# One written order of steps replaced by another in a gated recurrence with a feed-forward block

## The chip, the cores and the metric

The kernel runs on one core of a Trainium2 chip. Five engines work side by side, each through its own list of instructions in order: PE (matrix products), DVE and ACT (elementwise work, ACT also functions such as exp and sin), POOL (small elementwise work here) and SP, which issues nearly all DMA transfers. They wait for each other by semaphores. The metric is the time of one execution in microseconds (us); seven runs of the kernel before have a median of 464.03 us (462.85 to 464.76).

## The reference

Inputs are q, k, v and a complex gate (a_re, a_im) for 4 batches, 8 heads, 768 positions of 48 numbers. For each head a state of 48 x 48 complex numbers is carried over the positions; its output goes through a feed-forward block that closes with a layer norm and a second product.

```python
mag = np.sqrt(a_re * a_re + a_im * a_im)
scale = np.minimum(mag, 0.999) / (mag + 1e-06)
a_re_n, a_im_n = (a_re * scale, a_im * scale)
for t in range(S):
    new_re = ar * S_re - ai * S_im
    new_im = ar * S_im + ai * S_re
    S_re, S_im = (new_re + kv, new_im)        # kv: outer product of k[t] and v[t]
    y[:, :, t] = einsum('bhd,bhde->bhe', q[:, :, t], S_re)
# x: y as (3072, 384)
h = x @ w_in                                  # 3072 x 1024
sm = softmax(h); solu = h * sm
ln = (solu - mean) / sqrt(var + 1e-06) * g_ln
out = ln @ w_out                              # 3072 x 384
```

The weights w_in, w_out and the gain g_ln come as 64-bit floats and are converted on the core.

## The kernel before

The 768 positions are cut in six blocks of 128, and a block of one batch is a *chunk*: 24 chunks, numbered block by block. Two chunks that follow each other form a *group* (12 groups), which shares the preparation of the gates. Nothing in the kernel is a plain loop over engines' work: each piece of work is a named step (a small function that issues one to some hundred instructions), all steps are put in a dictionary `steps` under their name and number, and four written lists say in which order they are issued: `START`, then `EVEN` and `ODD` in turn for the chunks 2 to 19, then `END`. As each engine works through its instructions in the order of issue, the lists set the order on every engine, SP's queue of DMAs included. In the lists `up0:-1` is the step `up0` of the chunk before the current one, and `clamp:g2` that of the group two after the current chunk's. A step is taken out of the dictionary when it is issued; one that is already gone, or isn't there for this number, is passed over.

```python
for n in range(2, NC * B - 4):
    for s in (ODD if n % 2 else EVEN).split():
        nm, i = s.split(":")
        go(nm, n // GB + int(i[1:]) if i[0] == "g" else n + int(i))
```

The steps, by engine and with the line of their main instruction:

- Of a group, the size of the gate: `load_ar`, `load_ai` (SP, L649); `clamp` (DVE, L735); `inverse` (ACT, L740); `ratio`, `tangent` (DVE, L746 to L752); `square`, `secant`, `fourth` (ACT); `size` (DVE, L765); `eps` (ACT); `lnm` (DVE, L772) writes the logarithm `f_lr`; `total0/1` (PE, L777) sums it over the positions; `grow0/1`, `decay0/1` (ACT, L781, L784); `last` (SP, L788) takes the last row of the decays away as `f_ends`; `ends` (DVE and POOL), `turn_ends` (PE), `tot` (DVE). `ks0/1`, `qs0/1` (DVE) scale k and q.
- Of a group, the angle: `trig` (ACT loads tables), `angle` (ACT, L817), `on` (DVE, L822), `phase0/1` (PE, L831), `nearest0/1` (ACT), `part0/1` (DVE, L838, then ACT), `cos`, `sin` (ACT; `sin` also sends one row on by a DMA of SP), `exp` (ACT loads tables).
- Of a chunk: `k2`, `q2` (DVE, L881) double k and q with cos and sin; `kqb` (DVE, L890) and `kqt0` (SP, four DMAs, L895) turn them; chunks 0 and 1 are turned by PE and ACT instead (`kt`, `kT`, `qt`, `qT`). `score0/1` (PE, L937), `mask0` (DVE, L941), `values` (PE, L969), `carry` (PE, L977) and `add` (DVE, L986) give the output `f_y` and the next state.
- Of a chunk, feed-forward: `turned_x` (ACT), `up0/1` (PE, L1009), `exp0` (ACT, L1014), `solu0` (DVE, L1018), `blocks` (DVE, L1037) and `away` (SP, four DMAs, L1043) turn the result; chunks 0, 1, 2 and 23 are turned by PE and ACT (`zt`, `zT`). `centred`, `norm` (POOL), `spread` (ACT, L1054), `down0/1` (PE, L1068), `scale` (ACT, L1073), `store` (SP, L1078).
- Of the weights: `fetch` (SP, L680) brings one of 14 pieces (0 to 5 of w_in, 512 wide; 6 to 13 of w_out, 384 wide), `raised` (ACT) and `convert` (DVE) make 32-bit floats of it; `gain`, `mean` (PE) and `centre` (DVE) fold g_ln and the mean into w_out. `again` (SP) reads a piece once more and `inspect` (DVE) looks at it, for a check on the inputs' range. After `END` comes `verdict`, which gathers these checks in one flag.

Buffers bind the order too. Two PSUM banks in turn serve `total`, `phase`, `turn_ends` and the turns by PE; `values` and `carry` share one bank, which `turned_x` or `add` frees; `up` has one pair of banks, freed by `exp0` and `solu0`; `down` has one, freed by `scale`. The pieces of the weights share six buffers; the results of `kqb` and of `blocks` have one buffer each.

Of the kernel before, what the change touches and what calls it, by code (L numbers as in the profile page):

```python
# [512 lines left out]


START = """
load_ar:0 load_ai:0 clamp:0 fetch:8 fetch:2 fetch:0 fetch:1 inverse:0 ratio:0 raised:8 raised:2 tangent:0
square:0 secant:0 convert:2 size:0 fourth:0 eps:0 fetch:5 convert:8 raised:0 load_k:0 raised:1 lnm:0 total0:0
load_q:0 load_ai:1 convert:1 grow0:0 decay0:0 total1:0 ks0:0 decay1:0 grow1:0 convert:0 trig:0 angle:0 qs0:0
load_ar:1 last:0 fetch:13 raised:5 fetch:3 phase0:0 ks1:0 nearest0:0 convert:5 phase1:0 nearest1:0 part0:0
part1:0 ends:0 load_q:1 cos:0 sin:0 turn_ends:0 exp:0 fetch:4 clamp:1 k2:0 load_v:0 qs1:0 tot:0 kt0:0 q2:0  # L520
inverse:1 kT0:0 qt0:0 kt1:0 qT0:0 k2:1 raised:3 qt1:0 ratio:1 kT1:0 load_vr:0 qT1:0 raised:13 kt0:1 fetch:10
tangent:1 square:1 q2:1 score0:0 kT0:1 score1:0 qt0:1 secant:1 raised:4 convert:3 mask0:0 values:0 size:1
convert:13 qT0:1 turned_x:0 fetch:6 fetch:7 fourth:1 kt1:1 fetch:9 raised:6 convert:4 kT1:1 raised:9 load_ai:2
eps:1 carry:0 convert:6 fetch:12 raised:10 convert:9 load_vr:1 fetch:11 raised:7 qt1:1 up0:0 add:0 up1:0 lnm:1
qT1:1 convert:10 total0:1 total1:1 carry:1 exp0:0 gain:0 mean:0 decay0:1 score1:1 convert:7 load_k:1 grow0:1
solu0:0 add:1 decay1:1 qs0:1 grow1:1 score0:1 load_ar:2 trig:1 mean:1 angle:1 raised:12 ks0:1 phase0:1 load_k:2
last:1 phase1:1 ks1:1 mean:2 qs1:1 mask0:1 convert:12 nearest0:1 nearest1:1 raised:11 part0:1 part1:1 again:0
values:1 clamp:2 cos:1 mean:3 load_vr:3 ends:1 again:1 sin:1 turned_x:1 exp:1 mean:4 convert:11 again:4
inverse:2 zt0:0 k2:2 mean:5 q2:2 kqb:2 zT0:0 load_ai:3 kqt0:2 k2:3 mean:6 ratio:2 mean:7 tangent:2 q2:3 square:2
secant:2 turn_ends:1 zt1:0 centred:0 spread:0 centre:0 fourth:2 centre:7 load_q:2 up0:1 centre:5 centre:4 up1:1  # L530
zT1:0 score0:2 size:2 eps:2 again:2 kqb:3 exp0:1 load_ar:3 tot:1 kqt0:3 centre:1 score1:2 load_v:1 lnm:2
centre:3 total1:2 centre:6 total0:2 decay1:2 centre:2 norm:0 solu0:1 down0:0 grow0:2 inspect:2 again:6 grow1:2
decay0:2 inspect:0 again:8 zt0:1 trig:2 angle:2 zt1:1 centred:1 spread:1 zT0:1 down1:0 mask0:2 on:2 load_v:2
load_v:3 zT1:1 ks0:2
"""
# [24 lines left out]

# [650 lines left out]
```

## Time and profile before

| what | us |
|---|---|
| median of 7 runs (lowest to highest) | 464.03 (462.85 to 464.76) |
| the profiled execution | 462.84 |
| its span, first to last instruction | 461.0 |
| PE busy, share of the span | 408.0, 88% |
| DVE busy | 367.3, 80% |
| ACT busy | 283.6, 62% |
| POOL busy | 54.9, 12% |
| mean granted PE clock | 0.983 |
| SP's DMA queue: time of its packets, as a share of 16 engines' span | 67.9% |

The profile is of one execution. An instruction is named by engine, line and the tile that it writes (`f_o` by `down`, `f_h` by `up`, `f_y` by `values`, `f_L` by `total`, `f_d` by `carry`, `f_kb` by `kqb`, `f_zb` by `blocks`). Matrix products overlap, so PE counts as busy nearly always where it has work; the gaps tell more. The chain of work goes back from the last instruction to whatever released each step.

### The profile page before, as it was taken

How to read it: one execution, taken by the hardware profiler on the slowest of the kernel's cores; microseconds unless marked ns; L12 is line 12 of the kernel's file. 1: busy time of each engine (PE TensorE's matmuls, PEld its weight loads, DVE VectorE, ACT ScalarE, POOL GpSimd, SP SyncE). 2: the span in 40 equal slices, each digit the busy share in tenths (PEclk: the TensorE clock that was granted, in tenths of full speed). 3: DMA queues.
4: the chain of work that ended last, by engine and by line, in shares of the span. 5: the costliest groups of instructions: out<-in, count | busy, mean ns of one | idle time of the engine just before them, and what ended most of it. 6: DMA issues, size and time to landing. Idle time of an engine off the chain costs nothing.

```text
span 461.0 us, 11488 instructions
## 1 busy us (share of the span) xinstructions
PE 408.0 (88%) x4764; PEld 275.0 (60%) x4764; DVE 367.3 (80%) x507; ACT 283.6 (62%) x441; POOL 54.9 (12%) x141
## 2 busy tenths in 40 slices
PE   0257985999999999999999999999999999999992
PEld 0125443654566865875775676676676677667771
DVE  5889999595799799799799799799699798753310
ACT  4989966665666656657648648648647746521230
POOL 3000001111111110110111101101102011011110
PEclk9999988899999999999999999999999999999997
DMA  9878959959369858859659669569569566272200
GB/s 253 196 203 224 190 146 216 254 136 205 99 144 192 205 123 175 203 125 207 160 123 228 146 134 204 129 131 225 118 147 211 110 152 147 42 185 75 63 17 26
DMA packets 167709, 72.28 MB, mean 157 GB/s; under 512 B 142176, under 2 KB 155488, under 8 KB 167648
## 3 DMA queue, kind: packets, MB, share of 16 engines
q1 hardware_dynamic: 167504, 71.14, 67.9%
q8 instruction: 39, 0.64, 0.6%
q10 hardware_dynamic: 144, 0.33, 0.2%
q14 instruction: 22, 0.18, 0.1%
HBM read 38.87 MB, written 4.72 MB: 95 GB/s over the span
## 4 chain that ended last, share of the span: by engine, by line
DVE 43%; PE 39%; issue 7%; ACT 4%; DMA 4%; SPq 2%; DVEq 0%; POOL 0%; ACTq 0%
PE f_o L1068 17%; DVE f_kb L890 9%; PE f_y L969 5%; PE f_h L1009 5%; DVE f_kq L881 5%; PE f_L L777 4%; PE f_phase L831 4%; DVE f_zb L1037 4%; DVE f_z L1018 3%; DVE f_att L941 2%; DMA f_q<-in_q_dram 2%; DVE f_lr L772 2%; DVE f_state L987 2%; DVE f_ai L746 2%; PE f_d L977 2%
## 5 line engine op out<-in xcount | busy, mean ns | idle before, releaser
L1068 PE MATMUL f_o<-f_w_out,f_zT 128*128 128x384 f32 x384 | 135.2, 501 | 0.3 <-ACT f_zT L1031 0.3
L1009 PE MATMUL f_h<-f_w_in,f_xT 128*128 128x512 f32 x288 | 131.2, 600 | 0.0
L1068 PEld LDWEIGHTS f_o<-f_w_out,f_zT 128*128 128x128 f32 x384 | 111.2, 295 | 15.9 <-issue 4.3
L1009 PEld LDWEIGHTS f_h<-f_w_in,f_xT 128*128 128x128 f32 x288 | 52.8, 190 | 55.8 <-issue 52.9
L890 DVE STREAM_TRANSPOSE f_kb<-f_kq 128x1536 f32<-128x1536 f32 x22 | 51.6, 2347 | 0.4
L777 PE MATMUL f_L<-f_lr,f_mats 128*128 128x384 f32 x48 | 21.6, 575 | 29.7 <-DMA f_q<-in_q_dram 17.7
L755 ACT ACTIVATE f_ar<-f_x 128x768 f32<-128x768 f32 x12 | 10.1, 842 | 57.2 <-DVE f_x L752 57.1
L1018 DVE SCALAR_TENSOR_TENSOR f_z<-f_h,f_z 128x1024 f32<-128x1024 f32 x24 | 29.2, 1216 | 19.4 <-ACT f_z L1014 19.4
L1037 DVE STREAM_TRANSPOSE f_zb<-f_z 128x1024 f32<-128x1024 f32 x20 | 42.5, 2123 | 0.4
L1014 ACT ACTIVATE f_z<-f_h 128x1024 f32<-128x1024 f32 x24 | 24.4, 1018 | 24.0 <-PE f_h L1009 23.8
L969 PE MATMUL f_y<-f_att,f_v 128*32 128x128 f32 (+1 forms) x384 | 36.7, 275 | 2.1 <-DVE f_att L941 2.1
L838 DVE SCALAR_TENSOR_TENSOR f_f<-f_f,f_phase 128x384 f32<-128x384 f32 x24 | 13.1, 550 | 29.7 <-ACT f_f L834 29.7
L969 PE MATMUL f_y<-f_att,f_vr 128*32 128x128 f32 x384 | 36.5, 275 | 0.0
L937 PEld LDWEIGHTS f_score<-f_kqT 96*32 96x32 f32 x1536 | 28.9, 110 | 10.8 <-issue 10.3
L1054 ACT ACTIVATE f_z<-f_z,f_less 128x1024 f32<-128x1024 f32 x24 | 27.4, 1142 | 13.0 <-DVE f_zb L1037 5.5
L777 PEld LDWEIGHTS f_L<-f_lr,f_mats 128*128 128x128 f32 x48 | 9.0, 211 | 42.3 <-DVE f_lr L772 30.9
L937 PE MATMUL f_score<-f_kqT 96*32 96x64 f32 (+3 forms) x1536 | 31.9, 234 | 1.1 <-DMA f_kqT<-f_kb 1.1
L941 DVE TENSOR_TENSOR f_att<-f_score,f_mats 128x1024 f32<-128x1024 f32 x24 | 29.1, 1211 | 4.3 <-PE f_score L937 4.1
L969 PE MATMUL f_y<-f_kqT,f_state 96*32 96x128 f32 (+1 forms) x640 | 32.3, 272 | 0.0
L969 PEld LDWEIGHTS f_y<-f_att,f_v 128*32 128x32 f32 (+1 forms) x384 | 19.9, 102 | 16.2 <-DVE f_kq L881 6.1
L1003 ACT COPY f_xT<-f_y 128x384 f32<-128x384 f32 x24 | 11.5, 477 | 26.6 <-PE f_y L969 26.6
L1051 POOL TENSOR_SCALAR f_less<-f_sum 128x1 f32<-128x1 f32 x24 | 8.2, 343 | 152.5 <-DVE f_z L1018 152.4
(99 smaller groups left out, 640.4 us busy)
## 6 DMA issues: line engine op xcount, KB each, us to landing
f_kqT<-f_kb SPq DMA_DIRECT2D x88, 192.0 KB, 3.4
f_zT<-f_zb SPq DMA_DIRECT2D x80, 128.0 KB, 2.7
f_raw<-in_moe_w_out_dram SPq DMA_DIRECT2D x16, 384.0 KB, 4.0
f_raw<-in_moe_w_in_dram SPq DMA_DIRECT2D x12, 512.0 KB, 5.3
f_ar<-in_a_re_dram SPq DMA_DIRECT2D x12, 384.0 KB, 6.0
f_ai<-in_a_im_dram SPq DMA_DIRECT2D x12, 384.0 KB, 5.4
f_k<-in_k_dram SPq DMA_DIRECT2D x12, 384.0 KB, 4.2
f_q<-in_q_dram SPq DMA_DIRECT2D x12, 384.0 KB, 4.9
```

Of the source, the lines that this page charges most:

```text
L777: nc.tensor.matmul(out=ps, lhsT=tri, rhs=st["lr"][:, i * DM:(i + 1) * DM], start=True, stop=True)
L881: nc.vector.tensor_tensor(out=t, in0=T["cs", g][:, i * H:(i + 1) * H], in1=heads(T[nm, g][:, i]).unsqueeze(2).to_broadcast([P, H, 2, D]), ...
L890: nc.vector.transpose(out=t, in_=T["kq", c].rearrange("p n h (f j) -> p j (n h) f", j=3))
L937: nc.tensor.matmul(out=scores[r0:r0 + 32, x, r:], lhsT=QK[:, r // 32, x], rhs=QK[:, r // 32:, H + x], start=True, stop=True)
L941: nc.vector.tensor_tensor(out=st["att"].rearrange("p (i u) t -> p i u t", u=2), in0=scores.rearrange("p (i u) t -> p i u t", u=2), in1=mat ...
L969: nc.tensor.matmul(**product)
L1009: nc.tensor.matmul(out=st["h"][:, half * 512:(half + 1) * 512], lhsT=st["xT"][:, c * P:(c + 1) * P], rhs=w_in[:, c, half * 512:(half + 1) ...
L1014: nc.scalar.activation(out=st["z"], in_=st["h"], func=AF.Exp, accum_out=sums[:, n:n + 1])
L1018: nc.vector.scalar_tensor_tensor(out=st["z"], in0=st["h"], scalar=1.0, in1=st["z"], op0=OP.mult, op1=OP.mult, accum_out=st["sum"][:, 0:1])
L1037: nc.vector.transpose(out=st["zb"].rearrange("p s t c -> p s c t"), in_=st["z"].rearrange("p (c f s) -> p s c f", s=4, f=32))
L1054: nc.scalar.activation(out=st["z"], in_=st["z"], func=AF.Square, bias=st["less"], accum_out=st["sum"][:, 1:2])
L1068: nc.tensor.matmul(out=st["o"], lhsT=st["zT"][:, c] if n in SHORT else st["zT"].rearrange("p r t c -> p (r t) c")[:, :, c], rhs=w_out[:, c ...
```

## The change

The four lists are written anew. The functions of the steps, the buffers, the loop and the set of steps stay as they are: both orders issue the same 1173 steps. In the loop, the odd chunk now has the next even chunk's `values` and the next group's `phase` at its end, where these were at the start of the even chunk; `blocks` and `away` of a chunk are followed by its `down` later; `again` and `inspect` of all pieces stand in `ODD`, where they stood partly in `START` and partly in `EVEN`. `START` goes on to `values:2`, `score` of chunk 3 and `phase` of group 2, so that the loop begins and ends that much further on.

```diff
 START = """
-load_ar:0 load_ai:0 clamp:0 fetch:8 fetch:2 fetch:0 fetch:1 inverse:0 ratio:0 raised:8 raised:2 tangent:0
-square:0 secant:0 convert:2 size:0 fourth:0 eps:0 fetch:5 convert:8 raised:0 load_k:0 raised:1 lnm:0 total0:0
-load_q:0 load_ai:1 convert:1 grow0:0 decay0:0 total1:0 ks0:0 decay1:0 grow1:0 convert:0 trig:0 angle:0 qs0:0
-load_ar:1 last:0 fetch:13 raised:5 fetch:3 phase0:0 ks1:0 nearest0:0 convert:5 phase1:0 nearest1:0 part0:0
-part1:0 ends:0 load_q:1 cos:0 sin:0 turn_ends:0 exp:0 fetch:4 clamp:1 k2:0 load_v:0 qs1:0 tot:0 kt0:0 q2:0
-inverse:1 kT0:0 qt0:0 kt1:0 qT0:0 k2:1 raised:3 qt1:0 ratio:1 kT1:0 load_vr:0 qT1:0 raised:13 kt0:1 fetch:10
-tangent:1 square:1 q2:1 score0:0 kT0:1 score1:0 qt0:1 secant:1 raised:4 convert:3 mask0:0 values:0 size:1
-convert:13 qT0:1 turned_x:0 fetch:6 fetch:7 fourth:1 kt1:1 fetch:9 raised:6 convert:4 kT1:1 raised:9 load_ai:2
-eps:1 carry:0 convert:6 fetch:12 raised:10 convert:9 load_vr:1 fetch:11 raised:7 qt1:1 up0:0 add:0 up1:0 lnm:1
-qT1:1 convert:10 total0:1 total1:1 carry:1 exp0:0 gain:0 mean:0 decay0:1 score1:1 convert:7 load_k:1 grow0:1
-solu0:0 add:1 decay1:1 qs0:1 grow1:1 score0:1 load_ar:2 trig:1 mean:1 angle:1 raised:12 ks0:1 phase0:1 load_k:2
-last:1 phase1:1 ks1:1 mean:2 qs1:1 mask0:1 convert:12 nearest0:1 nearest1:1 raised:11 part0:1 part1:1 again:0
-values:1 clamp:2 cos:1 mean:3 load_vr:3 ends:1 again:1 sin:1 turned_x:1 exp:1 mean:4 convert:11 again:4
-inverse:2 zt0:0 k2:2 mean:5 q2:2 kqb:2 zT0:0 load_ai:3 kqt0:2 k2:3 mean:6 ratio:2 mean:7 tangent:2 q2:3 square:2
-secant:2 turn_ends:1 zt1:0 centred:0 spread:0 centre:0 fourth:2 centre:7 load_q:2 up0:1 centre:5 centre:4 up1:1
-zT1:0 score0:2 size:2 eps:2 again:2 kqb:3 exp0:1 load_ar:3 tot:1 kqt0:3 centre:1 score1:2 load_v:1 lnm:2
-centre:3 total1:2 centre:6 total0:2 decay1:2 centre:2 norm:0 solu0:1 down0:0 grow0:2 inspect:2 again:6 grow1:2
-decay0:2 inspect:0 again:8 zt0:1 trig:2 angle:2 zt1:1 centred:1 spread:1 zT0:1 down1:0 mask0:2 on:2 load_v:2
-load_v:3 zT1:1 ks0:2
+load_ar:0 load_ai:0 fetch:9 fetch:13 fetch:5 clamp:0 fetch:11 inverse:0 ratio:0 raised:9 raised:13 tangent:0
+fetch:2 convert:9 square:0 secant:0 size:0 fetch:0 load_k:0 raised:11 eps:0 convert:13 lnm:0 fetch:1 fourth:0
+total0:0 load_ar:1 raised:0 total1:0 raised:5 decay0:0 grow1:0 grow0:0 decay1:0 convert:11 trig:0 angle:0
+convert:5 convert:0 ks1:0 phase0:0 raised:2 phase1:0 last:0 ks0:0 load_q:0 nearest0:0 gain:0 nearest1:0 ends:0
+load_ai:1 load_v:0 convert:2 raised:1 part0:0 part1:0 fetch:7 cos:0 convert:1 qs0:0 turn_ends:0 tot:0 clamp:1
+sin:0 k2:0 exp:0 q2:0 kt0:0 inverse:1 kT0:0 qt0:0 fetch:3 k2:1 fetch:4 qs1:0 ratio:1 kt1:0 load_vr:0 qT0:0
+raised:7 kT1:0 qt1:0 qT1:0 q2:1 carry:1 kt0:1 score1:0 raised:3 fetch:10 convert:7 fetch:6 kT0:1 fetch:12 add:1
+fetch:8 raised:4 score0:0 load_k:1 mask0:0 load_ai:2 kt1:1 tangent:1 load_q:1 qt0:1 values:0 convert:3 qT0:1
+kT1:1 qt1:1 turned_x:0 carry:0 square:1 qT1:1 secant:1 up0:0 raised:6 convert:4 up1:0 raised:8 size:1 load_ar:2
+eps:1 score1:1 load_vr:2 fourth:1 raised:10 score0:1 convert:6 raised:12 convert:8 lnm:1 total0:1 convert:10
+grow0:1 decay0:1 total1:1 load_v:1 grow1:1 mean:0 convert:12 ks0:1 mean:1 mean:2 mean:3 decay1:1 mean:4 exp0:0
+mask0:1 mean:5 trig:1 qs0:1 angle:1 phase0:1 add:0 nearest0:1 phase1:1 solu0:0 nearest1:1 ks1:1 last:1 mean:6
+centred:0 qs1:1 mean:7 values:1 clamp:2 part0:1 part1:1 zt1:0 cos:1 sin:1 centre:0 exp:1 centre:1 load_k:2
+turned_x:1 zt0:0 centre:4 load_vr:1 centre:3 up0:1 inverse:2 up1:1 centre:2 centre:5 centre:7 zT0:0 k2:2
+centre:6 q2:2 ratio:2 spread:0 tangent:2 load_ai:3 zT1:0 kqb:2 square:2 secant:2 kqt0:2 down0:0 size:2 k2:3 q2:3
+down1:0 eps:2 exp0:1 load_q:2 lnm:2 fourth:2 total1:2 total0:2 kqb:3 solu0:1 grow1:2 decay1:2 kqt0:3 ends:1
+score0:2 centred:1 grow0:2 score1:2 decay0:2 turn_ends:1 tot:1 last:2 zt0:1 mask0:2 zt1:1 load_ar:3 values:2
+qs1:2 score0:3 score1:3 trig:2 angle:2 zT0:1 turned_x:2 on:2 ks1:2 zT1:1 mask0:3 phase0:2 norm:0 load_v:2
+spread:1 phase1:2 ks0:2 scale:0 qs0:2 nearest0:2
 """
 EVEN = """
-again:1 values:0 phase0:g1 phase1:g1 qs1:g1 norm:-1 turned_x:0 nearest0:g1 inspect:-1 carry:0 nearest1:g1 qs0:g1
-part0:g1 add:0 load_q:g2 score1:1 last:g1 again:8 scale:-2 part1:g1 score0:1 cos:g1 clamp:g2 sin:g1 exp:g1
-mask0:1 inverse:g2 up0:0 up1:0 load_vr:g1 exp0:0 k2:2 q2:2 kqb:2 load_v:g2 values:1 kqt0:2 ratio:g2 down0:-1
-solu0:0 zt0:0 turned_x:1 blocks:0 carry:1 down1:-1 tangent:g2 away:0
+nearest1:g1 mask0:1 carry:0 part0:g1 ks1:g1 load_q:g2 part1:g1 cos:g1 clamp:g2 up0:0 sin:g1 up1:0 load_k:g2
+add:0 exp:g1 values:1 inverse:g2 k2:2 exp0:0 down0:-1 q2:2 kqb:2 turned_x:1 ratio:g2 solu0:0 tangent:g2
+load_v:g2 square:g2 load_ar:g3 blocks:0 carry:1 secant:g2 size:g2 k2:3
 """
 ODD = """
-square:g2 secant:g2 fourth:g2 ks1:g1 ends:g1 up0:0 load_k:g2 k2:2 q2:2 score0:1 zT0:-1 score1:1 load_ai:g3
-zt1:-1 centred:-1 spread:-1 turn_ends:g1 size:g2 load_ar:g3 scale:-2 eps:g2 kqb:2 add:0 lnm:g2 tot:g1 mask0:1
-zT1:-1 up1:0 kqt0:2 norm:-1 exp0:0 total1:g2 grow1:g2 inspect:1 total0:g2 grow0:g2 store:-2 decay1:g2 solu0:0
-ks0:g2 decay0:g2 store:-3 trig:g2 angle:g2 blocks:0 centred:0 spread:0 on:g2 down0:-1 away:0 down1:-1
+kqt0:1 down1:-2 q2:2 eps:g2 load_ai:g3 up0:0 up1:0 add:0 fourth:g2 centred:-1 zt0:-1 zt1:-1 zT0:-1 away:-1
+norm:-2 scale:-2 again:-4 score0:1 zT1:-1 lnm:g2 store:-3 score1:1 exp0:0 spread:-1 kqb:2 solu0:0 total1:g2
+decay1:g2 total0:g2 decay0:g2 mask0:1 down0:-1 blocks:0 again:-3 ends:g1 grow0:g2 qs0:g2 load_vr:g2 down1:-1
+last:g2 kqt0:2 grow1:g2 centred:0 turn_ends:g1 values:1 trig:g2 inspect:-3 ks0:g2 angle:g2 score0:2 store:-2
+on:g2 spread:0 inspect:-6 tot:g1 score1:2 away:0 norm:-1 phase0:g2 qs1:g2 turned_x:1 scale:-1 phase1:g2
+nearest0:g2
 """
 END = """
-ks1:11 phase0:11 nearest0:11 values:20 norm:19 phase1:11 turned_x:20 part0:11 nearest1:11 score1:21 part1:11
-score0:21 mask0:21 qs0:11 cos:11 load_vr:11 sin:11 up0:20 exp:11 k2:22 scale:18 q2:22 up1:20 down0:19 kqb:22
-exp0:20 kqt0:22 solu0:20 blocks:20 centred:20 spread:20 values:21 turned_x:21 down1:19 norm:20 scale:19 qs1:11
-k2:23 score0:22 score1:22 q2:23 away:20 up0:21 kqb:23 up1:21 mask0:22 values:22 down0:20 kqt0:23 down1:20
-store:19 exp0:21 last:11 turned_x:22 store:18 scale:20 solu0:21 score0:23 score1:23 blocks:21 centred:21
-spread:21 mask0:23 away:21 up0:22 up1:22 values:23 store:20 down0:21 norm:21 exp0:22 solu0:22 turned_x:23
-blocks:22 centred:22 spread:22 down1:21 ends:11 scale:21 away:22 up0:23 up1:23 down0:22 down1:22 exp0:23
-store:21 solu0:23 norm:22 zt0:23 scale:22 zT0:23 zt1:23 centred:23 spread:23 down0:23 norm:23 zT1:23 down1:23
-store:22 scale:23 store:23
+mask0:21 down0:19 nearest1:11 store:18 part0:11 part1:11 cos:11 sin:11 norm:19 k2:22 up0:20 q2:22 up1:20 exp:11
+kqb:22 ks1:11 values:21 exp0:20 down1:19 solu0:20 turned_x:21 kqt0:22 score0:22 k2:23 q2:23 kqb:23 up0:21
+scale:19 blocks:20 kqt0:23 score1:22 up1:21 mask0:22 exp0:21 score0:23 centred:20 away:20 solu0:21 score1:23
+values:22 mask0:23 blocks:21 centred:21 spread:20 down0:20 turned_x:22 norm:20 up0:22 store:19 down1:20
+spread:21 scale:20 up1:22 exp0:22 values:23 away:21 down0:21 solu0:22 turned_x:23 ends:11 blocks:22 down1:21
+up0:23 norm:21 up1:23 away:22 scale:21 store:20 down0:22 centred:22 exp0:23 solu0:23 zt0:23 spread:22 centred:23
+zT0:23 store:21 down1:22 zt1:23 norm:22 scale:22 down0:23 zT1:23 spread:23 down1:23 norm:23 store:22 scale:23
+store:23
 """
```

## The prediction

> **What bounds the kernel now.** I read the page's busy table first, then the busy times of stretches cut at every fourth `f_L` matmul (step `total`), then the chain of work, then the SP queue in order of time. Busy shares alone do not settle it:
>
> ```profile
> PE 408.0 (88%) x4764; PEld 275.0 (60%) x4764; DVE 367.3 (80%) x507; ACT 283.6 (62%) x441; POOL 54.9 (12%) x141
> ```
>
> The stretches (columns: stretch, length, busy of PE, PEld, DVE, ACT, POOL, granted clock, DMA share, GB/s) split the run into a start, nine pairs of chunks, an end and a tail:
>
> ```profile
> 0.00:78.93 78.93, 42.93 (x451) 23.83 (x451) 67.52 (x119) 63.42 (x97) 6.19 (x18) 0.96 0.83 204
> 78.93:116.19 37.26, 34.96 (x369) 19.98 (x370) 27.42 (x40) 23.05 (x36) 5.46 (x11) 0.94 0.85 199
> 216.19:249.54 33.35, 32.67 (x417) 22.97 (x417) 30.17 (x41) 21.45 (x34) 5.11 (x11) 1.00 0.76 169
> 249.54:282.95 33.41, 32.67 (x417) 22.98 (x417) 30.22 (x41) 21.52 (x34) 3.77 (x11) 1.00 0.78 169
> 383.01:452.03 69.02, 68.70 (x610) 49.42 (x610) 32.33 (x42) 25.16 (x44) 7.87 (x25) 1.00 0.35 87
> 452.03:461.00 8.97, 0.12 (x2) 0.01 (x2) 0.29 (x2) 0.58 (x1) 0.00 (x0) 0.69 0.10 34
> ```
>
> In the start DVE works 67.5 of 78.9 us and PE only 42.9. A steady pair takes 33.35 us with 32.67 of PE. The end is PE without a break. The chain through one steady pair shows why 0.68 us of PE is lost each time:
>
> ```profile
> 248.62 0.88 DVE f_lr L772
> 249.50 0.04 issue
> 249.54 1.56 PE f_L L777 x4
> 251.10 5.16 PE f_o L1068 x16
> 256.26 1.90 PE f_y L969 x64
> 258.16 1.49 PE f_phase L831 x4
> 259.65 0.84 PE f_d L977 x48
> 260.49 0.02 issue
> 260.51 0.56 DVE f_state L986
> ...
> 282.95 1.56 PE f_L L777 x4
> ```
>
> It is a loop: PE from `total` to `carry` (10.95 us), then DVE without a pause from `add` to `lnm` (22.4), which frees the next `total`. Neither engine alone fills the pair; the order makes them hand over at two points.
>
> [...] Here PE shows 88% and its weight loads 60%, so I take as PE's floor of a pair its work at the pace measured where it doesn't wait, 32.67. [...] `f_L` at 78.93 came after 3.81 us without work, and four of its matmuls took 2.90 us there against 1.56 at 249.54. [...] before the `kqt0` at 268.80 the queue stands 3.27 us in its wait and issues nothing.
>
> **The change, part by part.** No instruction is added or removed: each order holds the same 1173 steps. What counts is what waits last.
>
> *A steady pair.* I projected the lists on the engines and laid the measured intervals (start of one step to start of the next, from the timeline of 238 to 272 us) one behind the other; t = 0 is `carry` of the even chunk. PE: carry 0.7, up 5.37, values 1.9, down0 2.9, carry 0.8, down1 2.8, up 5.37, score 1.25, total 1.45, down 5.25, turn_ends 0.15, values 1.9, score 1.25, phase 1.49: 32.6. Then each gate:
> - `values` (odd chunk) at t = 6.1 needs `mask0` (done about 0) and the `add` that frees the PSUM bank. DVE: part0, ks1, part1, clamp, add end at 3.9.
> - DVE goes on: k2, q2, kqb to 7.9 (the `sin` they need ends at 3.75 on ACT); ratio, solu0 to 11.0 (solu0 frees the bank for the second `up` at 14.5); tangent, blocks to 14.5; size, k2, q2, add, lnm to 19.0. `total` is due on PE at 21.1, so it no longer waits: 2 us of room where there were -0.7.
> - `away` is issued 14.5 to 17.0 and lands at about 19.9; `down` is due at 22.6. DVE: kqb, solu0, mask0, blocks to 25.8, ends, qs0, ks0, on, inspect, tot, qs1 to 29.5. DVE's sum is 30.4 of 32.6: no bound.
> - SP: `load_k`, `load_v` and `load_ar` now leave together after `sin` at t = 1.5 and flow at 1.9 us each until about 10; the first `kqt0`, issued at 8, lands behind them near 13 and is due at 20. Two `again` and a `store` (0.6 to 0.9 each) go out between 17 and 19, `load_vr` (2.2) by 21.3, in time in which SP waits anyhow; without that cover they would push `last` back one for one. On POOL `centred`, `norm` and `ends` (1.2 us a chunk) are needed by `spread` and `scale` on ACT, 2 to 6 us later; ACT's sum is 22 us, and its `exp0` starts only when `up` ends.
> - The tight gate is the second `kqt0`. It stands on SP behind `last`, which waits for both `decay` steps. These follow `total` (end 22.6): 0.2 to ACT, 0.45 the last decay, so `last` starts at 23.3. Its own issue is the unknown:
>
> ```profile
> 21.19 0.64 SPq L788 DMA_DIRECT2D f_ends<-f_ar  x1
> ...
> 258.15 0.44 SPq L649 DMA_DIRECT2D f_q<-in_q_dram  x1
> 258.69 2.54 SPq L788 DMA_DIRECT2D f_ends<-f_ar  x1
> ...
> 268.80 2.68 SPq L895 DMA_DIRECT2D f_kqT<-f_kb  x4
> ```
>
> It took 0.64 us with nothing large just sent, and 1.35 to 3.66 (median 2.6 of the nine in the loop) right behind a `load_q`; the `load_v` behind four `load_vr` took 0.45. Now `last` stands behind `load_vr` and I take 0.65. Then `kqt0` starts at 24.0, its fourth DMA at 25.9, and lands 3.5 to 4.1 us later (measured at 268.8 and 247.7): 29.4 to 30.0, and `score` is due at 29.9. I take 32.8 us a pair, 0.55 less than now; eight pairs from the `total` of group 3 to that of group 11 give 4.4.
>
> *The start.* DVE is the limit, so I count DVE up to `lnm:2`, which ends at 78.8. The new list moves `kqb:3` (2.26), `ends:1` (0.33) and `tot:1` (0.1) behind it, and three more `centre` (1.57) ahead: -1.1. The rest is waits. The old order has DVE gaps of 0.15 to 0.8 us between 13 and 30 us, because a 512-wide conversion (1.8 us of DVE, 1.45 of ACT) stood where ACT hadn't its bits. The new one takes 384-wide pieces first (1.5 and 1.25 us). Walking its list I get `q2:1` at 36.9, `lnm:1` at 49.9 (49.4 now, but with two more conversions and another add done), both `part` of group 1 at 60.2 and `lnm:2` at 75.5. DMA decides whether that holds: `fetch:8` must wait for the buffer that `convert:7` frees at about 38.4, and `load_k:1`, `load_ai:2`, `load_q:1`, `load_ar:2` queue behind it. At about 1.9 us each (landings 247.2, 249.1, 251.1 of three loads in a row) they land at 43 to 49; the first, `load_k:1`, is used at 53. `sin:1` then holds SP until 60; behind it are `load_k:2`, `load_vr:1`, `load_ai:3` and `kqt0:2`, needed from 72 on.
> PE: `up` of chunk 1 and both `down` of chunk 0 (5.2 us) now come ahead of `total:2`, in time in which PE stood still, at full clock since PE is busy from about 64. After `total:2` (75.6): `score` 2 at 77.4, `values` 2 at 80.7 (waits 0.8 for `mask0`), `score` 3 at 83.3 (waits for `kqt0:3`, 77.8 + 5.4), `phase` ends 86.0; then without a gap carry 0.75, up 5.4, values 1.0, down and carry 6.5, up 5.4, the turns of chunk 2 0.9, score 1.2: `total:3` at 107.1 against 116.2. That is 9.1 us.
>
> *The end.* PE does the same work, 69.0 us from `total:11`. New are two short waits: `kqb:23` ends about 14.9 us into END, its DMA lands at 20.3, and `score1:23` is due near 20: with `score0:22` about 0.7 together. The turns of chunk 23 stand between the halves of `down` 22 and hide the copy that now leaves 0.3 us. I take +0.5. The tail after the last `down`, 9.0 us, keeps its order.
>
> **Sum.** 461.0 - 9.1 - 4.4 + 0.5 = 448.0 us of span. The profiled execution took 462.84, 1.84 more than its span; the same offset gives 449.8. It lies 1.2 below the median of 464.03, so a median of 451.0.
>
> **Rivals.**
> - *The steady pair gains nothing* (another hand-over takes the place of `lnm` to `total`, or PE's pace between other neighbours is slower by 0.5 us). For it: PE has only 0.68 us of gap to give, and the gates listed above are within 4 us of their dates. Against: by the same walk none is late, and DVE comes 2 to 3.5 us ahead of each. It gives 451.0 + 4.4 = 455.4.
> - *`last` holds `kqt0`: slower than before.* If its issue takes x, the loop PE carry-to-total (22.6), decay 0.65, x, `kqt0` 5.5, score and phase 2.75 is 31.6 + x. At x = 1.2 it overtakes PE; at 2.6 a pair takes 34.2 and eight cost 6.8 against now, result about 462; from x = 2.8 the kernel is slower than before; at 3.66, the longest seen, about 471. For it: SP does stop behind large loads, and `again` and `load_vr` are just ahead. Against: they are spent by 23 us, when `last` may start.
> - *The start doesn't come early*: a load late behind `fetch:8` or `sin:1` keeps `total:3` at 116. Then only 4.4 - 0.5 is left, 460.1; 4 us of extra wait undo that too.
>
> The change does do what it says: the lists differ in all four parts.
>
> **Numbers.** My case 0.57 (447 to 454.5), steady gains nothing 0.18 (454 to 458), `last` 0.12 (0.05 at 458 to 463, 0.07 above 464), start 0.13 (457 to 464). Range 446.5 to 459.5: it takes in the first two whole, part of the others, and an error of 3 us either way in the walk through the start. A measurement here tells some 0.2% (0.9 us) from no change: faster 0.88, same 0.03, slower 0.09.
>
> **What would show it.** `total` of group 3 near 107 and of group 11 near 370; pairs of 32.6 to 33.0 us with PE busy over 99%; no wait of `f_L` for `f_lr`, and small ones of `f_score` for the landing of `f_kqT`; `f_ends` issues of 0.6 to 1 us in the loop; no clock under 1.0 between 64 and 445 us. The forecast is wrong if `f_ends` takes 2 us and more, if DVE in the start waits for `f_k` or `f_ai` from HBM, or if a PE wait of over 0.5 us returns in every pair.

## The result and the profile after

The changed kernel takes 460.58 us (median of 13 runs, 458.39 to 462.52); the kernel before, run beside it, 463.73. The ratio is 0.9936, with an interval of 0.9921 to 0.9952: faster by 3 us, where 13 were forecast. The profiled execution took 459.41 us, its span 457.6, so what lies around the span (1.81 us) is as before. The busy table of the kernel after hardly differs from that of before:

```profile
PE 407.1 (89%) x4764; PEld 277.6 (61%) x4764; DVE 366.7 (80%) x507; ACT 283.3 (62%) x441; POOL 50.9 (11%) x141
```

Its busy times by stretch, cut at the same `f_L` matmuls as before (columns: stretch, length, busy of PE, PEld, DVE, ACT, POOL, granted clock, DMA share, GB/s):

```profile
0.00:78.40 78.40, 46.67 (x401) 26.73 (x402) 66.52 (x117) 63.41 (x97) 4.72 (x14) 0.98 0.71 172
78.40:111.65 33.25, 30.17 (x418) 18.51 (x417) 26.40 (x34) 21.22 (x35) 4.10 (x11) 0.95 0.80 174
178.70:212.02 33.32, 32.61 (x423) 23.13 (x418) 30.35 (x40) 21.39 (x34) 4.11 (x11) 1.00 0.82 189
212.02:244.73 32.71, 32.60 (x422) 23.12 (x418) 30.30 (x40) 21.39 (x34) 4.10 (x11) 1.00 0.84 192
376.54:448.60 72.06, 69.45 (x615) 49.35 (x610) 33.09 (x46) 26.03 (x44) 9.49 (x29) 1.00 0.31 79
448.60:457.60 9.00, 0.02 (x1) 0.00 (x0) 0.29 (x2) 0.58 (x1) 0.00 (x0) 0.70 0.10 33
```

Up to the total of group 2 hardly anything is gained, the stretch after it is 4 us shorter, the pairs differ from each other, and the end is 3 us longer. Against the terms of the forecast, in us of span:

| stretch | before | after | difference | forecast |
|---|---|---|---|---|
| first instruction to total of group 3 | 116.19 | 111.65 | -4.54 | -9.1 |
| total of group 3 to group 11, eight pairs | 266.82 | 264.89 | -1.93 | -4.4 |
| total of group 11 to the last `down` | 69.02 | 72.06 | +3.04 | +0.5 |
| tail | 8.97 | 9.00 | 0.0 | 0.0 |

The first of these terms is the least certain: six profiles of kernels that share this START and its single buffer for `kqb` have the total of group 3 at 111.65 to 113.95, and that of the kernel after is the earliest. Below, *the end stretch* is that from the total of group 11 to the last `down`.

### The profile page after: what moved, and what is told of

The parts are those of the page before. It is cut to its first block, busy times and chain, and to the rows that moved or that the text cites. A ratio compares the mean times of both kernels' runs of the same rounds, so it can differ in the third digit from the quotient of the medians.

```text
span 457.6 us, 11496 instructions
## 1 busy us (share of the span) xinstructions
PE 407.1 (89%) x4764; PEld 277.6 (61%) x4764; DVE 366.7 (80%) x507; ACT 283.3 (62%) x441; POOL 50.9 (11%) x141
## 4 chain that ended last, share of the span: by engine, by line
issue 33%; PE 31%; DVE 10%; DMA 8%; ACT 8%; POOL 5%; SPq 4%; DVEq 0%; POOLq 0%; ACTq 0%
PE f_h L1009 11%; PE f_o L1068 10%; DMA f_kqT<-f_kb 7%; SPq L895 4%; PE f_y L969 3%; PE f_phase L831 2%; DVE f_kb L890 2%; PE f_score L937 2%; PE f_d L977 2%; POOL f_less L1051 1%; POOL f_rs L1062 1%; DMA f_ar<-in_a_re_dram 1%; ACT f_z L1014 1%; POOL f_s L1059 1%; ACT f_z L1054 1%
## 5 line engine op out<-in xcount | busy, mean ns | idle before, releaser
L1009 PEld LDWEIGHTS f_h<-f_w_in,f_xT 128*128 128x128 f32 x288 | 54.2, 192 | 63.9 <-issue 57.5
L1051 POOL TENSOR_SCALAR f_less<-f_sum 128x1 f32<-128x1 f32 x24 | 12.0, 499 | 358.8 <-DVE f_z L1018 300.7
L937 PE MATMUL f_score<-f_kqT 96*32 96x96 f32 (+3 forms) x1536 | 32.2, 235 | 6.4 <-DMA f_kqT<-f_kb 5.8
L969 PE MATMUL f_y<-f_att,f_v 128*32 128x128 f32 (+1 forms) x384 | 37.4, 280 | 0.4 <-DVE f_att L941 0.4
L777 PE MATMUL f_L<-f_lr,f_mats 128*128 128x384 f32 x48 | 20.0, 541 | 18.4 <-DVE f_lr L772 18.4
L755 ACT ACTIVATE f_ar<-f_x 128x768 f32<-128x768 f32 x12 | 10.1, 845 | 38.0 <-DVE f_x L752 22.3
L1073 ACT ACTIVATE f_ot<-f_o,f_rs 128x384 f32<-128x384 f32 x24 | 13.8, 577 | 19.0 <-PE f_o L1068 9.7
L834 ACT ACTIVATE f_f<-f_phase,f_bias 128x384 f32<-128x384 f32 x24 | 14.0, 582 | 18.2 <-PE f_phase L831 17.5
```

Source lines behind the costliest of these rows:

```text
L777: nc.tensor.matmul(out=ps, lhsT=tri, rhs=st["lr"][:, i * DM:(i + 1) * DM], start=True, stop=True)
L937: nc.tensor.matmul(out=scores[r0:r0 + 32, x, r:], lhsT=QK[:, r // 32, x], rhs=QK[:, r // 32:, H + x], start=True, stop=True)
L969: nc.tensor.matmul(**product)
L1009: nc.tensor.matmul(out=st["h"][:, half * 512:(half + 1) * 512], lhsT=st["xT"][:, c * P:(c + 1) * P], rhs=w_in[:, c, half * 512:(half + 1) ...
```

## The experiments

Each kernel was timed in five rounds beside the kernel before; ratios are to that.

**The steady pair: the place of `kqt0`.** What PE waited for between the totals of groups 3 and 11 in the kernel after (columns: who waited for whom, us in all, times, longest):

```profile
PE f_score L937 <- DMA f_kqT<-f_kb: 3.5, 5, 1.0
PE f_score L937 <- issue: 0.3, 1, 0.3
```

So the gate is the one that the forecast called tight. The first run changes only it:

```diff
 ODD
-last:g2 kqt0:2 grow1:g2
+kqt0:2 last:g2 grow1:g2
```

> The changed kernel with one pair of steps exchanged in ODD: kqt0 of the next odd chunk is issued before last, so that SP sends the four DMAs of f_kqT as soon as kqb has ended (about 0.3 us after the start of total) and not behind the wait for the decays. Theory A (the steady pair lost 0.5 us to f_kqT landing late behind last): the wait of f_score for f_kqT goes, the eight pairs from the total of group 3 to that of group 11 shrink from 33.11 to 32.6 to 32.75 us, the span from 457.6 to about 454.3. Rival B (another hand-over, mask0 to values or a bank of PSUM, is due at nearly the same time): the pairs stay above 33.0 and the span above 457. Rival C (f_ends now comes late for turn_ends of the same group): a wait of f_tot or of POOL's copy of 1 us or more appears on PE.

Measured: 453.06 us, ratio 0.9771 [0.9741, 0.9801]. All eight pairs take 32.40 us, `score` starts 8.58 us after `total` in each, and the list of PE's waits over them is empty. One of them:

```profile
178.38:210.78 32.40, 32.40 (x423) 23.18 (x418) 30.35 (x40) 21.39 (x34) 4.08 (x11) 1.00 0.84 193
```

PE's floor for a pair is therefore 32.40, not the 32.6 of the forecast's walk, and the place of `kqt0` behind `last` cost 0.71 us a pair, 5.7 of the 7.5 us gained here. (The end stretch is 0.6 us shorter too, and the tail 1.2 in this profile; these were not taken apart.) Why 33.1 and not 32.8? The SP queue of the kernel after, in two pairs, shows it (columns: start, duration, what is issued):

```profile
143.04 2.72 SPq L659 DMA_DIRECT2D f_vr<-in_v_dram  x4
147.36 0.58 SPq L788 DMA_DIRECT2D f_ends<-f_ar  x1
148.05 3.83 SPq L895 DMA_DIRECT2D f_kqT<-f_kb  x4
...
214.16 0.59 SPq L788 DMA_DIRECT2D f_ends<-f_ar  x1
214.86 2.64 SPq L895 DMA_DIRECT2D f_kqT<-f_kb  x4
```

`last` is issued 2.15 us after `total` (145.21 and 212.02) and takes 0.58, so the first `kqt0` starts 2.84 after `total`, as the walk had it (2.2, 0.65, 2.9). But the four DMAs of `kqt0` do not always follow each other evenly: in the first pair here they take 3.83 us to issue, where the walk had some 2.5, and the pair takes 33.49; in the second they take 2.64, and the pair 32.71. Over the nine times the fourth is issued 4.8 to 6.2 us after `total` and lands at 8.7 to 9.6; `score` is due at 8.58, by the walk at 8.8 (29.9 less 21.1). Two runs ask what holds the four. First `load_vr` alone was taken from ahead of `last`:

```diff
 ODD
-kqt0:1 down1:-2 ... ends:g1 grow0:g2 qs0:g2 load_vr:g2 down1:-1
+kqt0:1 load_vr:g2 down1:-2 ... ends:g1 grow0:g2 qs0:g2 down1:-1
```

> The changed kernel with `load_vr` moved from just ahead of `last` to just behind the first `kqt0` of ODD, some 14 us earlier; `kqt0` stays behind `last`. Theory A (kqt0 is late because it stands behind last, which starts 2.2 us after total whatever is ahead of it): score goes on waiting 0.4 to 1 us a pair, the eight pairs take 33.0 to 33.2 us in the mean, ratio 0.992 to 0.995. Theory B (kqt0 lands late because the four pieces of load_vr and the two re-reads ahead of it are still flowing): last is issued as before, but the landing of kqt0 comes 0.3 to 0.7 us earlier, pairs 32.5 to 32.8, ratio 0.985 to 0.990.

Measured: 460.31 us, 0.993 [0.991, 0.9951], pairs of 33.31 in the mean, `score` waiting 5.3 us for `f_kqT` over the eight. Theory B falls for `load_vr`. Then the re-reads went with it:

```diff
 ODD
-kqt0:1 down1:-2 ... scale:-2 again:-4 score0:1 ... blocks:0 again:-3 ends:g1 ... load_vr:g2 down1:-1
+kqt0:1 load_vr:g2 again:-4 again:-3 down1:-2 ... scale:-2 score0:1 ... blocks:0 ends:g1 ... down1:-1
```

> The changed kernel with both `again` and `load_vr` moved to just behind the first `kqt0` of ODD; `kqt0` stays behind `last`. In the trace of the changed kernel the four DMAs of the second kqt0 do not follow each other at 0.64 us in six of nine pairs: one of them is issued 0.4 to 1.3 us late, and one of them at 150.67, just as the eighth DMA before it, a re-read, lands (150.66). Theory A (these holds, and so the late landing, come from the re-reads that are still flowing ahead of kqt0): with the re-reads gone the four are issued at +2.84, 3.5, 4.1 and 4.8 us after total in nearly all pairs, land at +8.7 to 9.0, score waits under 0.4, pairs 32.6 to 32.8 us, ratio 0.985 to 0.990. Theory B (the holds come from something else on the queue, and kqt0 behind last is late whatever is ahead): pairs of 33.0 to 33.3, score waiting 0.4 to 1 us in most, ratio 0.992 to 0.995, as when load_vr alone was moved.

Measured: 468.62 us, 1.0143 [1.0096, 1.0191], slower than either theory has it. PE's waits from group 3 to 11 tell why:

```profile
PE f_o L1068 <- DMA f_zT<-f_zb: 6.5, 3, 2.8
PE f_o L1068 <- ACT f_ai L781: 2.7, 2, 1.4
PE f_score L937 <- DMA f_kqT<-f_kb: 1.5, 3, 1.0
```

`load_ai` and `away` now stand behind the re-reads, the turned result (`f_zT`) comes late, and pairs take 34.1 us in the mean. The wait of `score` falls from 3.5 to 1.5 us, but not because `kqt0` lands earlier, as theory A has it: over the eight pairs the fourth DMA is issued 5.1 us after `total` in the mean (5.3 in the kernel after) and lands at 9.1 in both kernels. In five of the eight PE now waits 1.3 to 2.8 us ahead of `score`, which so comes at 10.3 to 11.7; in the other three `score` still waits, 0.2 to 1.0 us. So the re-reads are not shown to be what makes `kqt0` late. What does stays open; to let `kqt0` pass `last` is what pays.

**The start: the one buffer of `kqb`.** The DVE instructions around the total of group 2 in the kernel after (in brackets: idle time before it, and who ended it):

```profile
76.67 0.96 DVE L772 SCALAR_TENSOR_TENSOR f_lr<-f_lr,f_u 128x768 f32<-128x768 f32 x1 [0.25 <-ACT f_u L769]
80.08 2.30 DVE L890 STREAM_TRANSPOSE f_kb<-f_kq 128x1536 f32<-128x1536 f32 x1 [2.45 <-DMA f_kqT<-f_kb]
```

`kqb:3` waits 2.45 us until the DMAs of `kqt0:2` have read the buffer; `tot:1`, which PE's turns need, stands behind it. The test gives `f_kb` two buffers, and pays for them by taking q and k from a pool with two buffers each instead of three:

```diff
-    natk, kbp = pool("f_natk", 2), pool("f_kb", 1)
+    natk, kbp = pool("f_natk", 2), pool("f_kb", 2)
-    load_q=load("q", q, ldv), load_k=load("k", k, ldv)
+    load_q=load("q", q, ld), load_k=load("k", k, ld)
```

> The changed kernel with two buffers for the result of kqb in place of one; the room is found by giving q and k two buffers instead of three, which no load waits for. Theory A (in the start kqb of chunk 3 stood 2.45 us for the one buffer, until the DMA of chunk 2 had landed, and all behind it on PE waited for its f_kqT): the gap of DVE before the second f_kb goes, f_kqT of chunk 3 lands at about 85.5 instead of 87.9, the total of group 3 comes at about 109.2 instead of 111.65 and the span falls to about 455.2. Rival B (mask0 of chunk 2 or the turns of chunk 1 were due as late): the total of group 3 stays at 111 or later.

Measured: 456.34 us, 0.9852 [0.9809, 0.9895]. The second `f_kb` starts without a wait, and from total to total PE is short of work for 0.7 us only:

```profile
76.69 2.29 DVE L890 STREAM_TRANSPOSE f_kb<-f_kq 128x1536 f32<-128x1536 f32 x1
...
78.84:108.21 29.37, 28.64 (x418) 17.33 (x416) 24.40 (x34) 20.99 (x34) 4.08 (x11) 1.00 0.86 187
```

That is 3.9 us less than in the kernel after (33.25), of which 1.5 is PE's own time: the granted clock of this stretch is 1.00 instead of 0.95.

**The start: what stands between total and total.** Both earlier edits together:

> Both earlier edits together: `kqt0` ahead of `last` in the loop, and a second f_kb buffer. Theory A (the missed buffer in the start and the place of `kqt0` behind `last` are two separate losses, one before the total of group 3 and one after it): they add. Total of group 3 at 108 to 108.6 (111.65 after the change, 113.6 with the swap alone), eight pairs of 32.4 us, total of group 11 at 367 to 368, span 447 to 448.5, ratio to before 0.966 to 0.971. Theory B (both take the same wait of score for f_kqT, so the second brings little on top of the first): total of group 3 near 110.5 to 113 because PE comes out of its pause at half clock all the same, span 450 or more, ratio 0.973 or more.

Measured: 447.55 us, 0.9656 [0.9634, 0.9679]: they add, as theory A has it, and a little more (13.0 us against 7.5 and 4.2 one by one). The profiled execution, the longest of the six (450.54), shows that the gate of group 3 is still near. The stretch in this profile, and in that of a kernel with the same start (`e7_all`, below):

```profile
78.16:111.36 33.20, 30.30 (x419) 18.49 (x417) 25.82 (x34) 21.02 (x34) 4.09 (x11) 0.95 0.81 174
...
78.52:108.02 29.50, 28.64 (x419) 17.33 (x417) 24.51 (x34) 21.08 (x34) 4.10 (x11) 1.00 0.86 188
```

In the first the last two DMAs of `kqt0:3` took 1.3 and 1.0 us longer from issue to landing, `score` waited 2.5 us instead of 0.5, and the granted clock was 0.95 instead of 1.00. PE has work at hand for such a gap, so I moved some into it:

```diff
 START
-values:2 qs1:2 score0:3 score1:3 trig:2 angle:2 zT0:1 turned_x:2 on:2
+values:2 qs1:2 turned_x:2 up0:2 up1:2 score0:3 score1:3 trig:2 angle:2 zT0:1 on:2
```

> The changed kernel with one move in START: both halves of `up` of chunk 2 (5.4 us of PE work, which EVEN did later) stand ahead of `score` of chunk 3, with `turned_x:2` ahead of them. Theory A (between the totals of groups 2 and 3 the loss is that PE stands still for the landing of the second `kqt0`, and then runs at half clock for some us): the wait of score for f_kqT goes, PE works 28.6 to 29 us there at a granted clock near 1.0 instead of 30.2 to 31.6, the wait of f_zt for f_ok (2.2 us) stays, and total of group 3 comes 31 to 32 us after that of group 2 (33.25 to 36.0 in the runs with this START). Ratio 0.985 to 0.991. Theory B (PE isn't what decides there; the total of group 3 hangs on DVE or a load): 33 us or more, ratio 0.992 to 0.995.

Measured: 463.10 us, 1.0003 [0.9985, 1.0021]: theory A falls. The wait of `score` is gone, but the total of group 3 comes at 115.58, 37.4 us after that of group 2:

```profile
PE f_y L969 <- DVE f_state L989: 2.7, 1, 2.7
PE f_zt L1028 <- DVE f_ok L802: 2.2, 1, 2.2
PE f_h L1009 <- ACT f_xT L1003: 0.6, 1, 0.6
```

`up` now stands ahead of `score` and `phase` on PE: `phase` starts at 94.15 instead of 89.34, with no gap before it since `up`. (`turned_x:2` also holds `angle` on ACT and `on` on DVE, but `on` is done at 90.6.) And `up` is missing where it stood: in the kernel after it runs on PE between `carry:2` and `values` of chunk 3, while DVE makes the new state in `add`. Here `values` follows `carry` and waits 2.7 us for that state, and the `down` behind it takes 4.5 us where the next one takes 2.85; the granted clock over the stretch is 0.91, against 0.95 in the kernel after. The last edit of this kind leaves `up` where it was and puts `phase` ahead of `score`:

```diff
 START
-... score0:3 score1:3 trig:2 angle:2 zT0:1 turned_x:2 on:2 ks1:2 zT1:1 mask0:3 phase0:2 norm:0 load_v:2
-spread:1 phase1:2 ks0:2 scale:0 qs0:2 nearest0:2
+... trig:2 angle:2 zT0:1 turned_x:2 on:2 ks1:2 zT1:1 phase0:2 norm:0 load_v:2 phase1:2
+score0:3 score1:3 ks0:2 qs0:2 nearest0:2 nearest1:2 part0:2 part1:2 spread:1 scale:0 mask0:3
```

> The changed kernel with one group of steps moved at the end of START: `phase` of group 2 stands ahead of `score` of chunk 3, `mask0:3` behind `part` of group 2, and `spread:1`, `scale:0` behind it on ACT. Theory A (the total of group 3 comes a fixed 21.4 to 23.6 us after the phase of group 2 starts, by a chain through ACT and DVE, and all that score 3 loses is lost because phase stands behind it): phase starts near 86.3, when `on:2` is done, instead of 89.4, and total of group 3 comes at 107.5 to 109 (111.65), whatever the landing of kqt0:3; ratio 0.983 to 0.989. Theory B (PE's own stall and half clock decide, so that the order of phase and score makes no difference): 111 to 113.5, ratio 0.992 to 0.995.

Measured: 458.34 us, 0.9888 [0.9866, 0.991]; `phase` starts at 85.44, total of group 3 at 109.51. The gain over the kernel after (2.2 us) is there, but theory A's fixed distance from `phase` isn't: it is now 24.1 us, and in that time PE has no gap over 0.2 us. From there on PE is the bound, with 28.6 to 29.0 us of work between the two totals.

**A new start with the old loop.** This was meant to price the start alone: the new START with EVEN, ODD and END of before; the re-reads and two looks that the old START held were appended to it.

> The new START with EVEN, ODD and END of the kernel before (the six re-reads and two inspections that the old START held are issued at its end). Theory A (the start gives 4.5 us by itself, whatever loop follows): total of group 3 at 111 to 113, pairs at 33.35, end at 69.0: span 456 to 457.5. Rival B (the old loop needs DVE to run ahead and gives part of it back): the first pairs take 34 us or more and the span is 458.5 or above.

Measured: 474.29 us, 1.0218 [1.019, 1.0246]. The pairs take 33.33 and the end stretch 69.0 us, as before the change, but it says nothing on the start alone, because DVE then stood 8.4 us at a look whose re-read was late (lines are one higher here):

```profile
100.08 1.87 DVE L703 TENSOR_REDUCE f_least<-f_raw 128x1 f32<-128x512 f32 x3 [8.40 <-DMA f_raw<-in_moe_w_in_dram]
```

**The end.** The kernel after with the END list of before:

> The changed kernel with the END list of the kernel before (steps already issued are passed over). Theory A (END's own order costs 3 us: f_kqT of chunk 23, f_zT of chunk 19 and the split halves): the stretch from the total of group 11 to the last down shrinks from 72.06 to 69.0 to 69.7 us, the span to about 454.8 to 455.2. Rival B (the waits come from the state in which the loop leaves SP and DVE): the stretch stays above 71 us.

Measured: 459.51 us, 0.99 [0.9874, 0.9927]; the end stretch takes 71.39 us. So the old list takes back 0.7 of the 3.0 us (PE busy 68.71 instead of 69.45), and the rest does not belong to END's list alone. Then the new END with three places mended (the scores of 22 behind `up` of 21, and together; both halves of `down` 20 together):

```diff
 END
-kqt0:22 score0:22 k2:23 q2:23 kqb:23 up0:21 ... kqt0:23 score1:22 up1:21 mask0:22 ... down0:20 turned_x:22 norm:20 up0:22 store:19 down1:20
+kqt0:22 k2:23 q2:23 kqb:23 up0:21 ... kqt0:23 up1:21 score0:22 score1:22 mask0:22 ... down0:20 down1:20 turned_x:22 norm:20 up0:22 store:19
```

> The changed kernel with only END's list changed in the three places (up of 21 ahead of score of 22, the two scores of 22 together, the two halves of down 20 together). Theory A (END's extra 3 us are two waits of score for f_kqT, one of down for away, and some 0.7 us of alternation): from the total of group 11 to the last down 69.5 to 70.5 us (72.06 after the change, 69.02 before), everything ahead of it unchanged, ratio 0.988 to 0.991. Theory B (the waits only move): 71.4 to 72.1, ratio 0.992 to 0.995.

Measured: 461.06 us, 0.9946 [0.9928, 0.9964]; the end stretch takes 72.3 us. Theory B: the waits moved. Of the kernel after, then of this one, PE's waits in the end stretch:

```profile
PE f_score L937 <- DMA f_kqT<-f_kb: 1.4, 2, 1.1
PE f_o L1068 <- DMA f_zT<-f_zb: 0.8, 1, 0.8
PE f_o L1068 <- ACT f_ot L1073: 0.4, 1, 0.4
```

```profile
PE f_score L937 <- DVE f_att L941: 1.4, 1, 1.4
PE f_o L1068 <- DMA f_zT<-f_zb: 1.3, 1, 1.3
PE f_o L1068 <- ACT f_ot L1073: 0.4, 1, 0.4
PE f_score L937 <- DMA f_kqT<-f_kb: 0.3, 1, 0.3
```

In the kernel after the 1.1 us are those of `score` of chunk 23, the other 0.4 those of chunk 21. Two scores in a row need `mask0` in between, so in the new list that of chunk 23 waits for `f_att`; its own `kqt0` had landed only 0.2 us before, so the wait for `f_kqT` was still there, hidden behind it.

**All together.** Swap, second buffer and this END:

> As the run before, with END's list changed in three places: both halves of `up` of chunk 21 stand ahead of `score` of chunk 22, both scores of 22 follow each other, and both halves of `down` 20 follow each other. Theory A (END's 3 us over before are waits of score for f_kqT and alternation between halves): from the total of group 11 to the last down 69.2 to 69.9 us instead of 71.4 to 72.1, no wait of score over 0.5 us there, span 445 to 446.5, ratio 0.961 to 0.967. Theory B (PE is bound by other waits there, as for f_zT or f_ot, which only move): 71 or more, ratio as in the run before.

Measured: 448.50 us, 0.9687 [0.9659, 0.9714]: the end stretch is 70.1 us and holds the same 1.4 us wait; no gain over swap and buffer. With `up` of chunk 2 moved, and `up1:21` between the scores of chunks 22 and 23:

> The swap of `kqt0` and `last`, the second f_kb buffer, the move of `up` of chunk 2 as in the run before, and END with `up0:21` ahead of both scores of 22 and `up1:21` between the scores of 22 and 23. Theory A: group 2 to group 3 29.2 to 29.8 us (29.5 and 33.2 in the two profiles with swap and buffer, which differed by when the last two DMAs of a kqt0 landed), eight pairs of 32.4, END 69.2 to 69.9 us, span 445 to 446, ratio 0.959 to 0.965. Theory B (the spread from 29.5 to 33.2 comes from something ahead of the total of group 2 or from DVE): group 3 spreads as before, ratio 0.966 to 0.969.

Measured: 451.91 us, 0.9754 [0.9729, 0.9779]: the total of group 3 at 112.53, with the same wait of 2.7 us for the new state as in the kernel with that move alone. With `phase` ahead of `score` instead, and END as changed:

> The same move together with the swap of `kqt0` and `last` and the second f_kb buffer; END as in the changed kernel. Theory A: phase of group 2 starts near 84.3, total of group 3 at 105.8 to 107 (108.0 and 111.4 in the two profiles with swap and buffer alone), eight pairs of 32.4 us, total of group 11 at 365 to 366.5, span 444 to 446, ratio 0.957 to 0.963. Theory B: total of group 3 at 108 to 111.4 as before, ratio 0.965 to 0.969.

Measured: 448.29 us, 0.9673 [0.965, 0.9695]; total of group 3 at 108.35, though `kqt0:3` landed as late in this profile (86.3) as in the one of swap and buffer in which the total came at 111.36 (86.0). So the move takes that gate away, but in the median it adds nothing to swap and buffer. These two have the lowest median, 447.55 us: 2.8% below the kernel after (0.9656 / 0.9936 = 0.972).

## Why the prediction was wrong

The direction was right, and so was the gate of the steady pair; all three terms of the sum were too hopeful, by 4.6, 2.5 and 2.5 us, which together is the 9.6 us between 451.0 and 460.58. The rival in which the start does not come early gives 460.1, near the measured time, but that is luck: the start did come earlier, and the other two terms did worse than it has them.

**The start, 4.5 instead of 9.1.** The walk has the total of group 2 at 75.6, the end of `phase` at 86.0 and the total of group 3 at 107.1; they came at 78.40, 90.90 and 111.65. Three steps failed.
- "The rest is waits": `lnm:2` was to end at 75.5 and ended at 77.63 (78.8 before). DVE's work ahead of it fell by 0.9 us, about as counted, but its waits did not fall. DVE's waits up to the total of group 2, before and then after:

```profile
DVE f_w_in L699 <- ACT f_bits L689: 1.4, 2, 0.8
DVE f_kq L881 <- ACT f_cs L848: 0.6, 1, 0.6
DVE f_lr L772 <- ACT f_u L769: 0.5, 1, 0.5
```

```profile
DVE f_w_in L699 <- ACT f_bits L689: 0.5, 2, 0.3
DVE f_att L941 <- PE f_score L937: 0.9, 1, 0.9
DVE f_lr L772 <- ACT f_u L769: 0.8, 2, 0.6
DVE f_lr L765 <- ACT f_u L758: 0.3, 1, 0.3
```

The narrower conversions saved the 0.9 us that the forecast saw, and `mask0:0` and the gate's chain took it back; with the lines that both share, DVE waits 8.9 us before and 8.9 after. The walk priced the waits that go, and not those that come. That these alone made `lnm:2` late is read from the trace, not tested.
- "at full clock since PE is busy from about 64" was the author's estimate. PE stood 3.34 us until 66.29, as `turned_x:1` stands behind `cos`, `sin` and `exp` on ACT, and `up` of chunk 1 then took 7.1 us instead of 5.4, at a granted clock of 0.76 over them. Both `down` of chunk 0 and the total follow without a gap:

```profile
66.29 7.11 PE L1009 MATMUL f_h<-f_w_in,f_xT 128*128 128x512 f32 x12 [3.34 <-ACT f_xT L1003]
...
78.40 1.45 PE L777 MATMUL f_L<-f_lr,f_mats 128*128 128x384 f32 x4
```

  So PE itself, not `lnm:2`, set the total of group 2. In the kernel with a second `f_kb` buffer `lnm:2` ended at 76.77, and that total came at 78.84 all the same. No run moved `turned_x:1`, so what it is worth stays open.
- "`score` 3 at 83.3 (waits for `kqt0:3`, 77.8 + 5.4)" took `kqb:3` to run from 75.5 to 77.8, without its single buffer. It waited 2.45 us there. A second buffer brought the total of group 3 forward by 3.4 us in the profiles (the medians differ by 4.2). The granted clock was under 1.0 here a second time (0.95 over the stretch to the total of group 3), against "no clock under 1.0 between 64 and 445 us".

**The steady pair, 0.24 us instead of 0.55.** The unknown, the issue of `f_ends`, came out as taken (0.58 for 0.65), and `kqt0` starts when it was to. The mis-sized term is the next, "its fourth DMA at 25.9": from the first to the fourth 1.9 us were taken, and the trace has 1.9 to 3.2; from the first issue to the last landing `kqt0` takes 5.9 to 6.7 us, where the walk has 5.4 to 6.0. With `score` due in the very window of the landing, each tenth counted. Two further errors of about 0.2 us hid each other: PE's own work is 32.40 and not 32.6, and `score` is due at 8.58 and not at 8.8. So where the four DMAs do follow each other evenly (fourth at 4.78, landings at 8.73 and 8.98), the pair takes 32.71 and 32.91, about the forecast's 32.8, in part by luck. This is the rival "`last` holds `kqt0`" in a mild form (its terms add up to 31.5 + x, not 31.6 + x): its loop was the binding one, though not through x but through its 5.5 us for `kqt0`. The rival that PE's own pace eats the gain falls: PE can do 32.40.

**The end, +3.0 instead of +0.5.** PE's waits there are 2.6 us, against 0.3 before, and its own busy time is 0.75 longer. Of the two waits named only that of `score` of chunk 23 came, with 1.05 us; chunk 22 did not wait. Not seen were 0.4 us of `score` of chunk 21, still the gate of the loop, 0.8 for `away` and 0.4 for `scale`. The step that failed is "PE does the same work, 69.0 us from `total:11`", the view that the end only inherits PE's work: it inherits the loop's order too. The kernel with the swap has the same END list, but the waits of 0.4 for chunk 21 and 0.8 for `away` are gone there, and PE is busy 68.97 us instead of 69.45. And the single `f_kb` buffer is a gate here as well: with the swap `kqb:23` waits 1.39 us for it, and the end stretch takes 71.4 us; with the second buffer added it waits for nothing, and the end takes 70.4.

```profile
397.34 2.27 DVE L890 STREAM_TRANSPOSE f_kb<-f_kq 128x1536 f32<-128x1536 f32 x1 [1.39 <-DMA f_kqT<-f_kb]
```

`phase` of group 11, its second half before and then all of it after:

```profile
392.20 0.91 PE L831 MATMUL f_phase<-f_x,f_mats 128*128 128x384 f32 x2
...
386.81 1.56 PE L831 MATMUL f_phase<-f_x,f_mats 128*128 128x384 f32 x4
```

Against the total of group 11 it ends 10.1 us later before and 11.8 after; `cos` needs both halves, and from there the chain goes on through `kqb:22` and `kqt0:22` to `score` of chunk 22. In the kernel with the old END list `kqt0:22` starts 20.5 us after that total, against 17.8 before, and `score` of chunk 22 waits 1.97 us. That the later `phase` is the cause was not tried by itself.

**Right:** the tail; the offset around the span; no wait of `f_L` for `f_lr` in the loop; waits of `f_score` for `f_kqT` as the sign to look for.

## What to carry to other kernels

In an order written by hand, walk each buffer with one copy as a gate of its own: "free" means that the DMAs which read it have landed (`kqb:3` waited 2.45 us for that). Where a step is due just when its transfer lands (here `score`, due 8.58 us after `total`, with landings from 8.7 to 9.6), the forecast of the transfer has to hold a spread, not a mean; two places swapped on the queue, so that the transfer on the critical loop goes first, gave more (7.5 us) than the whole new order (3). And work moved into a gap of one engine is missing where it stood, where it may have covered another engine's delay (here DVE's, 2.7 us).

## What was not expected of the hardware

- *A DMA waited for one issued long before that it has nothing to do with.* SP's waits in the kernel with `kqt0` ahead of `last`, groups 3 to 11, name re-reads of the weights as what `kqt0` waited for:

```profile
SPq L895 <- DMA f_raw<-in_moe_w_in_dram: 4.0, 4, 1.6
SPq L895 <- DMA f_raw<-in_moe_w_out_dram: 2.4, 4, 1.1
```

In each of these eight cases the re-read is the eighth DMA before it on the queue, and the issue follows its landing by 0.01 to 0.02 us (as at 150.82 after 150.80). In the kernel after it happened once, at 150.67 after 150.66. There none of SP's 351 DMAs is issued before the eighth ahead of it has landed, and at most eight are under way at once. Most of the other late issues in the kernel after (1.0 to 1.4 us in place of 0.6) have no such partner, and what held them stays open.
- *Half clock after a short pause.* In the kernel after, PE stood 2.17 us before `zt0:1`, and its eight products then took 1.94 us, at a granted clock of 0.50; after 1.16 us in the kernel with `phase` ahead they took 1.06, in a stretch (78.54 to 109.51) with a granted clock of 1.00:

```profile
82.56 1.06 PE L1028 MATMUL f_zt<-f_mats,f_z 128*128 128x128 f32 x8 [1.16 <-DVE f_ok L802]
```

In the kernel with the new START and the old loop they took 1.06 us too, although PE had stood 2.16 us before them. So the length of the pause alone did not decide; what did stays open. Of the six profiles with this START and the single `f_kb` buffer, three have a granted clock of 0.95 between the totals of groups 2 and 3, and the latter at 111.65 to 112.87. In the three that have it at 113.46 to 113.95, `zt0:1` took 1.94 us and `phase` 2.70 to 2.93 (1.94 and 1.56 in the kernel after), and PE had stood 2.0 to 2.2 us before `score` for the landing of `kqt0:3`, against 0.8 to 1.8.
- *PE's busy time was longer where PE had been stopped.* A pair counts 32.60 us of PE in the kernel after (212.02 to 244.73) and 32.40 in that with `kqt0` ahead of `last`, where it never waits, with the same products in the same order on PE.
